# Attention's first microseconds: clears written as 32-bit pairs, centroids scaled by ScalarE, and a new set of ranks for the planner

## The chip, the core and the metric

The kernel runs on one core of a Trainium2 chip. A core has five engines that run side by side, each with its own queue, which it works off in order: TensorE (PE in the profile; its weight loads are shown apart as PEld), VectorE (DVE), ScalarE (ACT), GpSimd (POOL) and SyncE (SP), which here issues the DMAs. The engines work on a memory called SBUF; TensorE writes its results to a second one, PSUM, from which VectorE and ScalarE copy them. The metric is the time of one execution on the device, in microseconds.

## What is computed

A clustered attention with 4 batches, 8 heads, 768 positions and 64 features, followed by a mixture of 8 experts on its output, with gates made doubly stochastic in eight rounds.

```python
q_assign = argmax(q_n @ c_n, -1)      # nearest of 16 centroids, per head
k_assign = argmax(k_n @ c_n, -1)
mask = q_assign[:, :, :, None] == k_assign[:, :, None, :]
scores = where(mask, scale * q @ k.T, -1e9)
attn = exp(scores - max(scores)); attn /= sum(attn) + 1e-9
x = (attn @ v)                        # 3072 x 512
P = exp(x @ w_gate - max)             # eight rounds of row and column normalising
out = sum over e of P[:, e] * (relu(x @ w1[e]) @ w2[e])
```

## The kernel before

Attention comes first and lasts until about 486 us; the experts fill the rest with a fixed, hand-written order on TensorE that the change does not touch.

Attention goes by pairs of heads, 16 in all. Per pair: q and k are loaded (`load_pair`), transposed by TensorE and copied out of PSUM (`split_part`, L630 and L638), the sum of magnitudes gives a scale (`scale_pair`, L654 on ScalarE or L656 on VectorE, then small VectorE steps L659 to L665), and each is split into a high and a low 16-bit half (`split_pair`, L679 or L681, and L683). `assign_pair` multiplies q and k with the scaled centroids (L702) and turns the nearest cluster into 16 extra rows of the operands qX and kX, so that two positions of different clusters get a large negative score. Small DMAs (`place_pair`) put the halves in place. Per head, `max_chunk` forms scores in nine chunks of 512 columns and VectorE takes the maxima (L849, L853), `max_rows` makes rows of them, and `exp_chunk` forms the scores again with the maxima subtracted (L945, L946), ScalarE exponentiates (L952) and GpSimd adds up (L970). `values` multiplies with v (L1004), `norm` divides.

The upper 64 partitions of qX and kX, into which those extra rows go, must be filled before: with zero for q, with -32768 for k. There are 16 such buffers of 64 x 768 16-bit numbers. `clear` writes one on GpSimd (L421), or `clear_rest` does it on ScalarE (L461); `blank` zeroes seven other tiles (L448 on GpSimd, L450 on ScalarE). The same process loads ScalarE's table for the exponential by a dummy activation (L465) after the first four clears. Before the planner starts, the centroids are loaded, their norm is taken (L354 to L362, with a square root on ScalarE, L359 and L360), and VectorE scales them into both halves of `cs` (L365), which TensorE transposes (L373) and VectorE copies to `cm` (L377). Casts of the identity matrix for later transpositions are L205 and L207.

The order of attention's work is made when the program is built. A `Planner` holds, for each engine, the time at which it is free, and processes (Python generators) that ask for an engine and a duration, or for one of several (engine, duration, reluctance). At each step it looks for the step with the smallest start plus reluctance; among the steps of that engine that could start within the engine's PATIENCE of it, the one with the smallest key goes first. Keys come from `urgency`: nine per head, plus the stage's number in KEYS. The order that comes out is fixed on each engine; the true times are the chip's.

```python
start = max(w.time + self.latency(w.engine, on), self.free.get(on, 0.0))
...
steps.append((start, start + (o[2] if len(o) == 3 else 0.0), w.key, i, w, o, on))
...
first = min(steps, key=lambda x: x[1:4])
```

Of the kernel before, what the change touches and what calls it, by code (L numbers as in the profile page):

```python
# [8 lines left out]
F32 = mybir.dt.float32  # L9
# [4 lines left out]
AF = mybir.ActivationFunctionType  # L14
ALU = mybir.AluOpType
# [4 lines left out]
SHIFT = 2.0**15  # L20
# [40 lines left out]
class Planner:  # L61
# [3 lines left out]

    LATENCY = 0.2
    SHARING = ("POOL", "DVE+")
    PATIENCE = {'PE': 0.0, 'ACT': 0.0, 'POOL': 0.26, 'SP': 0.0, 'DVE': 0.0}

    def __init__(self, tc):  # L70
        self.tc = tc
# [58 lines left out]
    def run(self):  # L130
        while True:
# [16 lines left out]
            engine = first[6]  # L148
            last = first[1] + self.PATIENCE.get(engine, 0.0)
            start, _, _, _, w, cost, _ = min((x for x in steps if x[6] == engine and x[1] <= last), key=lambda x: (x[2], x[1], x[3]))  # L150
# [14 lines left out]
def attn_moe_kernel(  # L165
# [11 lines left out]
    nc = tc.nc  # L177
    B, H, S, D = q.shape
# [29 lines left out]
    ones = const.tile([P, P], F32, name="ones")  # L208
# [20 lines left out]
    PE, ACT, DVE, POOL, SP, DVE2 = "PE", "ACT", "DVE", "POOL", "SP", "DVE+"  # L229
# [104 lines left out]
    with ExitStack() as actx:  # L334
# [16 lines left out]
        cn = nat.tile([P, D], F32, name="cn", bufs=1)  # L351
# [3 lines left out]
        cnorm = sm.tile([P, 1], F32, name="cnorm", bufs=1)  # L355
        nc.vector.tensor_reduce(out=cnorm, in_=csq, axis=AX, op=ALU.add)
        root = sm.tile([P, 1], F32, name="root", bufs=1)
        begun = sm.tile([P, 1], F32, name="begun", bufs=1)
# [3 lines left out]
        nc.vector.reciprocal(cnorm, cnorm)  # L362
        cs = nat.tile([P, 2, D], F32, name="cs", bufs=1)
        for x in range(2):
            nc.vector.tensor_scalar(out=cs[:, x, :], in0=cn, scalar1=cnorm, scalar2=None, op0=ALU.mult)  # L365
        cm = const.tile([P, NP, 2, C], F32, name="cm")
        nc.vector.memset(cm.rearrange("p a x c -> p (a x c)"), 0.0)

# [47 lines left out]
        for nm, i in last:  # L416
            t = (pers if (nm, i) in kept else brief).tile([P, 2, S], F16, name=f"{nm[0]}{i}")
            for j in range(2):
                bufs[nm[j]].append(t[:, j, :])
        def clear(nm, t):  # L420
            nc.gpsimd.memset(t[64:128, :], -SHIFT if nm[0] == "k" else 0.0)  # L421


        def buffers(p):
# [17 lines left out]
        def blank(*ts):  # L442
            for t in ts:
                t = t if len(t.shape) == 2 else t.rearrange("p a b -> p (a b)")
                n = t.shape[1]
                e = yield (ACT, 0.08 + n * 0.00083), (POOL, 0.1 + n * 0.00083, RELUCT[10])
                if e == POOL:
# [2 lines left out]
                    nc.scalar.activation(t, ones[:, 0:1].broadcast_to([P, n]), AF.Copy, scale=0.0)  # L450

        def clear_rest():
            yield 6.0
            for i in range(NB):
                for nm, ts in bufs.items():
                    if "X" in nm and i < len(ts):
                        e = yield (ACT, 0.72), (POOL, 0.73, RELUCT[10])
                        if e == POOL:
                            clear(nm, ts[i])
                        else:  # L460
                            nc.scalar.activation(ts[i][64:128, :], ones[64:128, 0:1].broadcast_to([64, S]), AF.Copy, scale=-SHIFT if nm[0] == "k" else 0.0)  # L461
                ev["clear", i].set(plan)
                if i == 0:
                    yield ACT, 1.5
                    nc.scalar.activation(begun, begun, AF.Exp, scale=0.0)  # L465
                if i == 1:
                    yield from blank(nhs[0], ves[0], nhs[1])
                    ev["clear", "first"].set(plan)
            yield from blank(nhs[2], ves[1], *rrs, spread.rearrange("p t x d -> p (t x d)"))
            ev["clear", "rest"].set(plan)  # L470
            yield DVE2, 0.3
            three12 = sm.tile([3 * R, R], F32, name="three12", bufs=1)
            nc.vector.tensor_tensor(out=three12, in0=ident[0 : 3 * R, 0:R], in1=ident[0 : 3 * R, R : 2 * R], op=ALU.add)
            nc.vector.tensor_tensor(out=three12, in0=three12, in1=ident[0 : 3 * R, 2 * R : 3 * R], op=ALU.add)
            yield ACT, 0.75
            nc.scalar.copy(
                spread[0 : 3 * R], three12.rearrange("r (x i) -> r i x", x=2).unsqueeze(3).broadcast_to([3 * R, NT, 2, D])
            )
            ev["spread"].set(plan)
# [3 lines left out]
        xq_from, xs_from = ({n: next(free) for n in ns} for ns in (XQ, XS))  # L483
        NCH = len(CHUNKS)
        plan = Planner(tc)
        plan.free.update({PE: 5.0, ACT: 4.0, DVE: 6.3, POOL: 3.0, SP: 1.0})

        KEYS = dict(load=-99.6, scale=-39.4, hilo=-210.9, split0=-186.4, split1=-28.7, split2=-30.4, assign=-39.2, place=-336.7, chain=-64.9, ones=-461.5, max=-25.1, rows=-30.6, exp=0, values=64.8, out=6.0, batch=29.5, group=76.9, vsum=-28.1, group0=-123.5, inputs=-41.6, first=1000)
        NL = 32
        GATES = [0, 0, 1, 0]  # L490
        COSTS = [0.66, 0.46, 0.432, 0.214, 0.42]
        RELUCT = [4.75, -0.72, 2.33, 16.21, 0.34, 0.01, 0.02, 5.4, -0.46, 3.06, 0.07]

        FIRST = ("load", "split0", "split1", "split2", "scale", "hilo", "assign", "place", "chain", "ones", "max", "rows")

        def urgency(stage, n, c=0):
            return n * NCH + c + KEYS[stage] - (KEYS["first"] if n == 0 and stage in FIRST else 0)

# [954 lines left out]
    sink, making, scanning, inputs = gates(), iter(()), iter(()), iter(())  # L1453
# [3 lines left out]
    with ExitStack() as ax:  # L1457
# [124 lines left out]
        for t in range(NI):  # L1582
            e, f2 = divmod(t, NP2)
# [11 lines left out]
            if t == 8:  # L1595
                inputs = next_x(1, True)
# [263 lines left out]
    inputs = iter(())  # L1860
    for n in range(NS + 1):
        one = layer1b(n) if n < NS else iter(())
        two = layer2b(n - 1) if n else iter(())
        if n < NS:
            b, e = slots[n]
            if e == 1 and b + 1 < B:
                inputs = next_x(b + 1)
# [37 lines left out]
```

## Time and profile before

| | us |
|---|---|
| median of 3 runs | 2281.86 (2281.69 to 2282.4) |
| the profiled execution | 2279.16 |
| its span, first to last instruction | 2277.1 |
| TensorE busy in the span | 2236.1 |
| VectorE, ScalarE, GpSimd busy | 1649.1, 1143.1, 1118.1 |

A line of the profile names the line of the kernel, the engine, the operation, and what it writes and reads. A wait is put down to the event that came last. The chain of waits follows the work that ended last back in time, from each instruction to the one that released it.

### The profile page before, as it was taken

The page shows a single profiled execution, that of the slowest core. Times are in us where ns is not written, and L with a number is a line of the kernel's source. Part 1 is how long each engine was busy: PE and PEld are TensorE (multiplying, and loading weights), DVE is VectorE, ACT ScalarE, POOL GpSimd, SP SyncE. Part 2 cuts the span into 40 slices and gives each one's busy share as a digit, 9 for nine tenths or more (in the row PEclk, how much of TensorE's full clock was granted, in tenths as well). Part 3 has the DMA queues.
Part 4 walks back from the last instruction along what each step waited for, and adds up shares of the span by engine and source line. Part 5 has one row for each costly group of instructions (what it writes and reads, how often), then busy time and mean ns, then how long its engine had stood idle before and what let it go on. Part 6 is the DMA issues. An engine that isn't in the chain of part 4 may idle for free.

```text
span 2277.1 us, 39662 instructions
## 1 busy us (share of the span) xinstructions
PE 2236.1 (98%) x15491; PEld 1458.8 (64%) x15491; DVE 1649.1 (72%) x2777; ACT 1143.1 (50%) x2107; POOL 1118.1 (49%) x997
## 2 busy tenths in 40 slices
PE   6999999999999999999999999999999999999999
PEld 3455554445555555567777777777777777777777
DVE  7988878567666766588788877776676666666667
ACT  7777786555666665354444443333433333333333
POOL 3676787854555655276666653233332332322223
PEclk7999999999999999999999999999999999999999
DMA  5345453365555543586766765544444554434433
GB/s 128 88 101 159 103 142 98 124 218 198 186 168 190 190 139 111 203 300 210 223 218 218 239 219 169 176 144 132 151 156 141 182 170 139 131 130 132 138 130 102
DMA packets 226860, 369.78 MB, mean 162 GB/s; under 512 B 73800, under 2 KB 163824, under 8 KB 226160
## 3 DMA queue, kind: packets, MB, share of 16 engines
q1 hardware_dynamic: 226240, 365.67, 50.3%
q8 instruction: 121, 1.98, 0.4%
q10 hardware_dynamic: 432, 1.57, 0.2%
q14 instruction: 67, 0.55, 0.1%
HBM read 272.22 MB, written 80.62 MB: 155 GB/s over the span
## 4 chain that ended last, share of the span: by engine, by line
PE 91%; DVE 6%; ACT 2%; issue 1%; DMA 1%; SPq 0%; DVEq 0%; ACTq 0%
PE h_ps L1387 38%; PE pb L1805 12%; PE pa L1805 8%; PE pc L1805 8%; PE av_ps L1004 4%; PE o_ps L1547 4%; PE o_ps L1549 4%; PE o_ps L1548 4%; PE exp_ps L945 2%; PE max_ps L849 2%; PE exp_ps L946 2%; DVE mrt L853 2%; PE misc_ps L1045 1%; PE misc_ps L630 1%; ACT pe L952 0%
## 5 line engine op out<-in xcount | busy, mean ns | idle before, releaser
L1387 PEld LDWEIGHTS <-wa 128*128 128x128 f16 x5376 | 525.6, 98 | 302.8 <-issue 5.3
L1805 PEld LDWEIGHTS <-ho 128*128 128x128 f16 x5940 | 580.8, 98 | 137.2 <-DVE ho L1700 1.1
L1387 PE MATMUL h_ps<-xsT,wa 128*128 128x384 f16 x3072 | 581.6, 326 | 1.2 <-DVE xsT L324 0.6
L1387 PE MATMUL h_ps<-xsB,wa 128*128 128x384 f16 x2304 | 436.9, 326 | 1.4 <-DVE B L1401 0.6
L1681 POOL TENSOR_TENSOR B<-B,B 128x768 f32<-128x768 f32 x96 | 197.9, 2064 | 468.2 <-DVE ho L1700 426.6
L1700 DVE TENSOR_TENSOR ho<-B,ho 128x768 f16<-128x768 f32 x283 | 348.1, 1230 | 1.6 <-ACT ho L1696 1.6
L1851 ACT ACTIVATE B<-B 128x384 f32<-128x384 f32 x288 | 149.7, 520 | 371.3 <-DVE B L1401 370.0
L1805 PE MATMUL pb<-w2o,ho 128*128 128x256 f16 x2532 | 322.2, 273 | 0.0
L1401 DVE SCALAR_TENSOR_TENSOR u<-h_ps,m 128x384 f32<-128x384 f32 x256 | 141.7, 553 | 243.5 <-PE h_ps L1387 240.7
L1696 ACT CAST ho<-B 128x768 f16<-128x768 f32 x283 | 226.8, 824 | 14.1 <-POOL B L1681 13.4
L970 POOL TENSOR_TENSOR psum<-psum,pe 128x512 f32<-128x512 f32 x160 | 208.1, 1317 | 43.6 <-ACT pe L952 40.3
L853 DVE TENSOR_REDUCE mrt<-max_ps 128x1 f32<-128x512 f32 (+1 forms) x288 | 188.8, 683 | 41.0 <-PE max_ps L849 39.7
L1805 PE MATMUL pc<-w2o,ho 128*128 128x256 f16 x1692 | 215.7, 273 | 0.3
L1805 PE MATMUL pa<-w2o,ho 128*128 128x256 f16 x1692 | 215.1, 273 | 0.0
L1681 POOL TENSOR_TENSOR B<-B,T 128x768 f32<-128x768 f32 x48 | 95.6, 1991 | 206.0 <-DVE ho L1700 206.0
L952 ACT ACTIVATE pe<-exp_ps 128x512 f32<-128x512 f32 x288 | 164.8, 597 | 56.9 <-PE exp_ps L946 51.2
L1411 ACT ACTIVATE m<-h_ps 128x384 f32<-128x384 f32 x128 | 62.6, 489 | 191.6 <-PE h_ps L1387 190.8
L1849 ACT ACTIVATE B<-h_ps 128x384 f32<-128x384 f32 x96 | 47.1, 490 | 211.4 <-PE h_ps L1387 211.4
L1549 PE MATMUL o_ps<-wb,hl 128*128 128x512 f16 x384 | 145.5, 379 | 0.0
L1548 PE MATMUL o_ps<-wb,hh 128*128 128x512 f16 x384 | 145.5, 379 | 0.0
L1547 PE MATMUL o_ps<-wb,hh 128*128 128x512 f16 x384 | 145.5, 379 | 0.0
L1610 ACT ACTIVATE hh<-c 128x384 f16<-128x384 f32 x128 | 66.9, 523 | 143.2 <-DVE c L1401 142.0
(281 smaller groups left out, 3280.8 us busy)
## 6 DMA issues: line engine op xcount, KB each, us to landing
wa<-w1d SPq DMA_DIRECT2D x98, 896.0 KB
w2o<-w2d SPq DMA_DIRECT2D x168, 512.0 KB
raw<-in_moe_w SPq DMA_DIRECT2D x60, 512.0 KB
w1d<-wa SPq DMA_DIRECT2D x30, 896.0 KB
r<-in_moe_w SPq DMA_DIRECT2D x32, 512.0 KB
w2d<-w2s SPq DMA_DIRECT2D x32, 512.0 KB
w2d<-wb SPq DMA_DIRECT2D x96, 128.0 KB
scan<-in_moe_w SPq DMA_DIRECT2D x32, 256.0 KB
```

The costliest lines, as they stand in the source:

```text
L853: nc.vector.tensor_reduce(out=t["mr"][:, i0 : i0 + ni, ni - 1], in_=ps.rearrange("p (x c) -> p x c", x=ni), axis=AX, op=ALU.max)
L952: nc.scalar.activation(pe, ps.rearrange("p (x c) -> p x c", x=ni), AF.Exp, scale=SCALE)
L970: (nc.gpsimd if e == POOL else nc.vector).tensor_tensor(out=st[:, o : o + N0], in0=old[o], in1=part, op=ALU.add)
L1387: nc.tensor.matmul(ps[:, 0:HB], wa[:, w_, a, c, :], x[:, x_, c, :], start=(first and s_ == 0), stop=(s_ == len(steps) - 1), skip_group_che ...
L1547: nc.tensor.matmul(po[i], hh[:, t, ti], wbh[:, t], start=(first and t == 0), stop=False)
L1548: nc.tensor.matmul(po[i], hh[:, t, ti], wbl[:, t], start=False, stop=False)
L1549: nc.tensor.matmul(po[i], hl[:, t, ti], wbh[:, t], start=False, stop=(last and t == 1))
L1681: nc.gpsimd.tensor_tensor(out=t, in0=d[a], in1=d[c], op=ALU.subtract)
L1696: nc.scalar.copy(t[:, 0], blocks[n, g][o])
L1700: nc.vector.tensor_tensor(out=t[:, 1], in0=blocks[n, g][o], in1=t[:, 0], op=ALU.subtract)
L1805: nc.tensor.matmul(ps[q], h[:, h_, f, q * P : (q + 1) * P], w[:, 2 * g + f, w_], start=(first and g == 0 and s_ == 0 and q % 2 == 0), stop ...
L1851: rests.append(lambda: nc.scalar.activation(c, c, AF.Relu))
```

## The change

- The clears of qX and kX write 384 32-bit numbers where they wrote 768 16-bit ones. Their value for k is the 32-bit number whose two halves are both -32768.
- The two scalings of the centroids move from VectorE to ScalarE, and the dummy activation that loads the exponential's table moves from `clear_rest` to a place right behind them.
- `clear_rest` no longer begins with a delay of 6.0 in the plan's time, and the durations that it asks for are shorter.
- The planner is given other times at which ScalarE, VectorE and GpSimd are first free, another PATIENCE, other KEYS and other reluctances. RELUCT[10] is that of GpSimd for the clears and blanks, [2] that of VectorE for the sums of L970, [4] and [5] those of ScalarE and VectorE for the high halves, [6] that of VectorE for the magnitudes, [7] that of VectorE for the copies out of PSUM, [8] and [9] those of VectorE and GpSimd for the sums of v.

```diff
-    PATIENCE = {'PE': 0.0, 'ACT': 0.0, 'POOL': 0.26, 'SP': 0.0, 'DVE': 0.0}
+    PATIENCE = {'PE': 0.01, 'ACT': 0.16, 'POOL': 0.28, 'SP': 0.0, 'DVE': 0.15}
...
         for x in range(2):
-            nc.vector.tensor_scalar(out=cs[:, x, :], in0=cn, scalar1=cnorm, scalar2=None, op0=ALU.mult)
+            nc.scalar.activation(cs[:, x, :], cn, AF.Copy, scale=cnorm)
+        nc.scalar.activation(begun, cs[:, 1, 0:1], AF.Exp, scale=0.0)
...
+        PAIR = -(2.0**113) * (1 + 0xF800 / 2.0**23)
+        assert SHIFT == 2.0**15
+
         def clear(nm, t):
-            nc.gpsimd.memset(t[64:128, :], -SHIFT if nm[0] == "k" else 0.0)
+            nc.gpsimd.memset(t[64:128, :].bitcast(F32), PAIR if nm[0] == "k" else 0.0)
...
         def clear_rest():
-            yield 6.0
             for i in range(NB):
                 for nm, ts in bufs.items():
                     if "X" in nm and i < len(ts):
-                        e = yield (ACT, 0.72), (POOL, 0.73, RELUCT[10])
+                        e = yield (ACT, 0.42), (POOL, 0.38, RELUCT[10])
                         if e == POOL:
                             clear(nm, ts[i])
                         else:
-                            nc.scalar.activation(ts[i][64:128, :], ones[64:128, 0:1].broadcast_to([64, S]), AF.Copy, scale=-SHIFT if nm[0] == "k" else 0.0)
+                            nc.scalar.activation(
+                                ts[i][64:128, :].bitcast(F32), ones[64:128, 0:1].broadcast_to([64, S // 2]), AF.Copy, scale=PAIR if nm[0] == "k" else 0.0
+                            )
                 ev["clear", i].set(plan)
-                if i == 0:
-                    yield ACT, 1.5
-                    nc.scalar.activation(begun, begun, AF.Exp, scale=0.0)
...
-        plan.free.update({PE: 5.0, ACT: 4.0, DVE: 6.3, POOL: 3.0, SP: 1.0})
+        plan.free.update({PE: 5.0, ACT: 6.2, DVE: 6.2, POOL: 2.7, SP: 1.0})
 
-        KEYS = dict(load=-99.6, scale=-39.4, hilo=-210.9, split0=-186.4, split1=-28.7, split2=-30.4, assign=-39.2, place=-336.7, chain=-64.9, ones=-461.5, max=-25.1, rows=-30.6, exp=0, values=64.8, out=6.0, batch=29.5, group=76.9, vsum=-28.1, group0=-123.5, inputs=-41.6, first=1000)
+        KEYS = dict(load=324.0, scale=-43.9, hilo=-165.9, split0=-88.0, split1=-58.3, split2=-42.9, assign=-26.7, place=-255.2, chain=-60.4, ones=-533.3, max=-24.1, rows=-117.3, exp=0, values=56.1, out=18.8, batch=-218.8, group=210.8, vsum=-143.1, group0=-194.2, inputs=-302.1, first=1000)
...
-        RELUCT = [4.75, -0.72, 2.33, 16.21, 0.34, 0.01, 0.02, 5.4, -0.46, 3.06, 0.07]
+        RELUCT = [32.96, -4.19, 3.07, -0.21, 0.33, 3.81, 1.36, 0.59, 0.16, 5.81, -8.55]
```

## Rows read from the trace of the kernel before

**Rows 1.** The page's first part: busy time, share, instructions of TensorE.

```profile
PE 2236.1 (98%) x15491; PEld 1458.8 (64%) x15491; DVE 1649.1 (72%) x2777; ACT 1143.1 (50%) x2107; POOL 1118.1 (49%) x997
```

**Rows 2.** Busy time by stretch; the stretch and its length come first.

```profile
core 0: us, PE busy (x) PEld busy (x) DVE busy (x) ACT busy (x) POOL busy (x), PEclk, DMA share, GB/s
...
8.00:40.50 32.50, 20.09 (x80) 9.13 (x79) 26.84 (x60) 23.82 (x41) 0.91 (x4) 0.64 0.44 100
40.50:60.00 19.50, 18.40 (x115) 9.99 (x114) 13.30 (x25) 17.13 (x34) 14.16 (x15) 0.98 0.65 145
60.00:160.00 100.00, 94.79 (x625) 49.66 (x625) 87.74 (x171) 74.37 (x175) 70.11 (x85) 1.00 0.39 93
160.00:200.00 40.00, 39.10 (x254) 20.76 (x253) 39.06 (x76) 30.44 (x72) 30.89 (x38) 1.00 0.63 166
200.00:486.00 286.00, 278.00 (x1833) 138.02 (x1832) 210.57 (x403) 199.78 (x477) 216.77 (x261) 1.00 0.42 117
```

**Rows 3.** The timeline from 0 to 14: start, duration, engine, line.

```profile
2.24 1.57 ACT L461 ACTIVATE qX<-ones 64x768 f16<-64x768 f32 x2
...
2.67 4.13 POOL L421 MEMSET qX<- 64x768 f16 x6
...
3.84 0.20 ACT L360 ACTIVATE root<-cnorm 128x1 f32<-128x1 f32 x1
...
4.46 2.42 DVE L365 TENSOR_SCALAR cs<-cn,cnorm 128x64 f32<-128x64 f32 x2
...
4.79 2.16 DVE L205 CAST ident_h<-ident 128x128 f16<-128x128 f32 x1
...
6.85 0.77 POOL L448 MEMSET nht<- 128x768 f32 x1
...
7.27 1.06 PE L630 MATMUL misc_ps<-ident,qn 128*128 128x128 f32 x4
...
8.08 0.44 DVE L377 COPY cm<-misc_ps 64x64 f32<-64x64 f32 x2
...
9.13 1.49 PE L630 MATMUL misc_ps<-ident,kn 128*128 128x128 f32 x6
```

**Rows 4.** The chain of waits up to 41: shares by line, then pieces.

```profile
by line: ACT qX L461 14.0%; DVE mrt L853 8.7%; DVE cs L365 5.9%; PE max_ps L849 4.8%; PE misc_ps L630 4.7%; ACT qn L638 4.7%; DVE qH L683 4.5%; ACT nht L450 3.6%; ACT L359 3.1%; ACT L465 3.1%; DVE qX L758 2.7%; PE misc_ps L702 2.7%; issue 2
...
10.23 1.28 ACT L465
...
11.52 0.20 ACT begun L465
...
12.87 0.59 ACT kn L638
...
13.51 1.09 PE misc_ps L702 x6
...
16.27 0.74 ACT nht L450
...
40.48 0.43 PE exp_ps L945
```

**Rows 5.** Line 638: duration in ns (least, median, most), first and last start.

```profile
L638 ACT COPY qn<-misc_ps x32: 344/489/606, 8.4 to 337.7; 128x512 f32<-128x512 f32 x16, 128x256 f32<-128x256 f32 x16
...
L638 ACTq EVENT_SEMAPHORE  x17: 17/17/17, 5.2 to 319.0; - x17
```

**Rows 6.** Instructions by line up to 486: busy us, mean ns, idle before.

```profile
L853 DVE TENSOR_REDUCE mrt<-max_ps 128x1 f32<-128x512 f32 (+1 forms) x288 | 188.8, 683 | 41.0 <-PE max_ps L849 39.7
...
L656 DVE TENSOR_REDUCE am<-qn 128x1 f32<-128x768 f32 x7 | 6.6, 946 | 4.8 <-ACT qn L638 4.8
...
L1131 DVE COPY gt<-misc_ps 96x256 f32<-96x256 f32 x3 | 1.3, 421 | 3.1 <-PE misc_ps L1125 3.1
...
L421 POOL MEMSET qX<- 64x768 f16 x6 | 4.1, 731 | 0.1
```

**Rows 7.** Who waited for whom on TensorE, 40 to 486: us, times, longest.

```profile
PE max_ps L849 <- DVE mrt L853: 5.0, 11, 1.4
```

## The prediction

> **What bounds the kernel now.** I read the page's first part first [rows 1]: TensorE is busy for 2236.1 of 2277.1 us. The table of stretches says where most of the other 41 us lie [rows 2]: from 8 to 40.5 it is busy 20.09 of 32.5 us, and before 8 there is hardly a matmul in the timeline [rows 3]; from 40.5 to 486, where attention ends, it is busy 430.3 of 445.5. Everything later is a fixed order on a full TensorE, and the diff leaves it alone. So the change is worth what it moves the point at which TensorE fills up, the first exponential chunk, at 40.48 in the chain of waits [rows 4], plus or minus what the new ranks do to the 15.2 us still idle between there and 486.
>
> Then the timeline of the start [rows 3] and the chain up to 41 us [rows 4]. ScalarE is the engine to watch: of those 41 us the chain passes 14.0% through its clears L461 (5.7 us), 3.1% through the exponential's table L465 (1.3 us, and 0.20 for the activation behind it), 3.31 us through six pieces of its blanks L450 (the first stands in the rows), and 5.9% through VectorE's scaling of the centroids L365 (2.4 us). That is 12.9 us of work on which no result of this stretch depends directly, or that is long only because it stands blocked. GpSimd, meanwhile, is busy for 0.91 of 32.5 us between 8 and 40.5 [rows 2]. VectorE is the next in line: 26.84 of the same 32.5 us, so 5.7 us idle.
>
> **The change, part by part.**
>
> Centroids. The reader sees two delays in [rows 3]: the root L360 stands behind two clears on ScalarE (2.24 to 3.84), and then both L365 need 2.42 us, since they start at 4.46 inside GpSimd's row of clears and end at 6.88, just after the row's end at 6.80. Afterwards ScalarE has no clears to do: root right after the sum of squares (about 3.0), two small VectorE steps (0.4 in all, from 4.04 to 4.46 before), two ScalarE copies of 128x64, each between the 0.20 of the 128x1 root and the 0.59 of a copy of 512 columns; I take 0.25, near the former, whose size is nearer. The scaled centroids are there at about 4.1 in place of 6.88. TensorE's queue begins with their transposition, and q's transpositions stand behind it (7.27); q has landed at 5.2, when the first of ScalarE's waits for a load is over [rows 5]. So q starts 2.0 us earlier, bounded by its landing, and 0.7 of the 2.8 us are lost to that.
>
> Table. L465 (1.28 + 0.20) leaves the chain at 10.23 and goes behind the copies, 4.1 to 5.6. It is hidden there by q's landing and its four transpositions, which end at about 6.3; without that cover it would cost 1.5. In this trace the next activation starts 0.01 us after the load [rows 4]. The Trainium skill (ScalarE: Activation LUTs, What ACT_TABLE_LOAD costs) gives 1283 ns for the load, with which the trace agrees, and another 1380 ns of drain, which it does not show; with that the first copy of q would be some 0.7 us late and the sum 5.8 in place of 6.5.
>
> Clears and blanks. In the planner's choice an engine's start counts plus its reluctance; at -8.55 GpSimd is preferred for all of them, because the process that issues them is one behind the other and never finds ScalarE 8.55 us ahead. So ScalarE loses 10 clears and 7 blanks. GpSimd's cost goes by elements, not bytes: 768 columns took 0.73 us as 16 bits [rows 6] and 0.77 as 32 bits [rows 3], so 384 pairs cost about 0.38. Sixteen are 6.1 us; three blanks of 768 columns and smaller ones of some 1.0 us in all are 3.3. GpSimd is busy from 2.67 to about 12.1 and has nothing else to do until the first rows' end.
>
> What that row of writes does to VectorE is this change's danger. The cast L205, queued at 4.79, ended at 6.95 [rows 3]. The six clears of 0.73 [rows 6] took 4.13 together, so each starts before the one before has ended, and nothing of VectorE's gets in between; the blank L448, of another shape, starts at 6.85, after a short pause, and the three waiting VectorE instructions passed there. Afterwards this pause comes after eight short clears, at 2.67 + 8 x 0.38 = 5.7. The casts (a second one follows) pass there, the small ones behind them take 0.4, and VectorE copies the transposed centroids at about 6.2 in place of 8.08. The Trainium skill (SBUF — State Buffer, Who interferes with whom) says that the one that starts first holds the shared ports for its whole instruction and the other blocks fully. By that sentence alone a cast would slip in after one clear, at about 4; this trace shows that it waits for three of them. Copies at 4.6 in place of 6.2 would help little, as k is not there yet: some 0.3 us, and the sum would be 6.8.
>
> The sum. *Up to the raw q and k*: on the chain between 8.37 and 15.7 stand two clears and the table, 0.84 + 0.84 + 1.48 = 3.2 us [rows 4]. With the 2.0 before them that would be 5.2. But k has to land: its time is not shown, it lies between 5.2, since it is issued behind q, and 9.1, when TensorE used it [rows 3]; I take 7, the middle. Then k's transpositions, copies and the rest end at about 10 in place of 13.46: 3.5 us. *From there to 40.5*: what is left of the 12.9 on the chain are clears and blanks of 5.8 us. What is late next is VectorE: it has 5.7 us idle in the whole stretch. Some of it belongs to the wait for q and k that is already counted, and some stays, since the first head's maxima go to and fro between VectorE and a TensorE that is partly at 1.2 GHz (0.64 of 2.4 granted on the mean from 8 to 40.5, 0.98 after [rows 2]). I take 3.0, about half. Together 6.5: the first exponential at about 34.
>
> Bounds: below, VectorE idles as much as before and only starts 1.9 us earlier; above, all 12.9 less 0.5 for the copies, if the second pair's VectorE work (some 5 us done before 40.5) is left for later. TensorE's clock came up where it got dense; it should do so that much earlier, which is in the sum.
>
> Ranks and patience from 40.5 to 486. They touch all of attention, and no row of before prices an order. The idle TensorE time there is 15.2 us; a better order gains no more, a worse one may lose as much. The reluctances shift work: copies out of PSUM, all on ScalarE now (32 of q [rows 5], and as many of k), become cheap for VectorE (5.4 to 0.59), sums of magnitudes (7 of q's 16 on VectorE [rows 6]) and the high halves become dear there. These roughly balance, so I take 0 and carry 4 either way into the range. Loads fall far back (-99.6 to 324) on SP's queue, behind the placing DMAs; they run pairs ahead, so nothing waits for a few us.
>
> The profiled execution took 2279.16 us (span 2277.1), 2.7 under the median of 2281.86. 2279.16 - 6.5 = 2272.7; against the median, 2275.4.
>
> **Rivals.**
> *The lock.* GpSimd's row has no pause that VectorE can use until 12.1; casts, centroid copies and all behind them start at 12.2. For it: the cast of before ended only with the row. Against it: the pause at 6.80. The assignment, which ended at 14.6 before [rows 4], waits for the centroids until 12.8, and with its 8 matmuls ends hardly sooner; nothing is left of the 3.5, and the lighter ScalarE still gives some 2: 2280, no change.
> *VectorE becomes the bound*, the one that ends slower. It has 87.7 of 100 and 39.06 of 40 us from 60 to 200 [rows 2]. A copy of 512 columns lies between the 0.42 of a 256-column one and the 0.68 of a 512-column reduction [rows 6]; both sizes for both inputs are about 2 us a pair, and a pair's copies come every 21 us (8.4 to 337.7 for 16 pairs [rows 5]). If most copies go to VectorE with little taken off it, two pairs' 4 us fill its 5.7 idle ones before 40.5, so the start gains nothing, and 13 us in 60 to 200 meet 13.2 idle ones. From there on every maximum makes TensorE wait: about 6 us, 2288. Against it: the magnitudes and high halves that leave.
> *Given back.* The start gains 6.5, and the new order leaves TensorE waiting that much more up to 486: most likely where it waits now, for the maxima (5.0 us [rows 7]), 2281, no change. For it: the ranks change everywhere; against: TensorE is 97% busy there under either.
>
> **How the numbers follow.** Forecast 0.60, lock 0.13, VectorE bound 0.13, given back 0.14. What a measurement of this kernel can tell from no change is about 0.2%, 4.6 us. The forecast's own range is 2270 to 2279; nine tenths of it gain over 4.6. The range for all is 2268 (12.4 and a little of the order) to 2283, which leaves out the VectorE case and the tail of the forecast. Faster 0.55, within 0.2% 0.31 (the rest of the forecast, the lock, most of what is given back), slower 0.14.
>
> **What would show it.** No clear or blank on ScalarE, 16 clears of about 0.38 us on GpSimd; scaled centroids at about 4, table load before 6; q's transpositions at 5.3; centroid copies at about 6 (12 is the lock); the first exponential at 33 to 36; TensorE's busy time from there to attention's end as before, with 15 us idle. If VectorE is over 95% busy from 60 to 200, or copies sit on it in numbers, it is the second rival; an early first exponential with an unmoved end of attention is the third.

## The result, and the profile of the changed kernel

The changed kernel takes 2293.93 us (median; 2291.11 to 2297.4) where the kernel before, timed beside it, takes 2282.4 (2281.69 to 2284.11). The ratio is 1.0051, 95% interval 1.0036 to 1.0066: slower by half a per cent, where I had forecast 2275.4 and a gain. The profiled execution took 2297.4 us (span 2295.6), the longest of its kernel, and that of before 2279.16, a short one. So the two traces lie 18 us apart and the medians 11.5; what follows explains the 18, and about a third of it is the two executions.

The page's first part shows the same instructions on TensorE as [rows 1] and 12.0 us more of its time.

```profile
PE 2248.1 (98%) x15491; PEld 1462.2 (64%) x15491; DVE 1656.1 (72%) x2777; ACT 1141.4 (50%) x2106; POOL 1116.9 (49%) x1009
```

The beginning came as forecast. The timeline of the changed kernel (start, duration, engine, line) answers [rows 3]:

```profile
2.66 2.93 POOL L425 MEMSET qX<- 64x384 f32 x8
...
3.50 2.18 DVE L205 CAST ident_h<-ident 128x128 f16<-128x128 f32 x1
3.62 0.59 ACT L365 ACTIVATE cs<-cn,cnorm 128x64 f32<-128x64 f32 x2 [0.42 <-DVE cnorm L362]
...
4.22 1.28 ACT L366 ACT_TABLE_LOAD   x1
...
5.53 1.11 PE L632 MATMUL misc_ps<-ident,qn 128*128 128x128 f32 x4 [0.74 <-DMA qn<-in_q]
5.65 0.77 POOL L452 MEMSET nht<- 128x768 f32 x1
...
6.16 0.44 DVE L378 COPY cm<-misc_ps 64x64 f32<-64x64 f32 x2
```

ScalarE has no clear left, eight clears take GpSimd 2.93 us, the centroids are scaled at 3.62 to 4.21, the table's load ends at 5.50 and q's transpositions start at 5.53, VectorE's casts end in GpSimd's pause at 5.68, and the centroid copies stand at 6.16 (8.08 before). The first exponential's matmul, by the instructions that write its tile (count, least, median and longest ns, first and last start), first in the changed kernel, then in the kernel before:

```profile
L947 PE MATMUL exp_ps<-qH x192: 269/376/634, 33.4 to 483.8; 128*128 128x512 f16 x96, 128*128 128x256 f16 x96
```

```profile
L945 PE MATMUL exp_ps<-qH x192: 269/330/634, 40.3 to 470.9; 128*128 128x512 f16 x96, 128*128 128x256 f16 x96
```

33.4 us in place of 40.3: 6.9 us sooner. The same query for the first product of expert 0's second layer, in the same order:

```profile
L1549 PE MATMUL o_ps<-wb,hh x384: 376/379/379, 512.8 to 972.8; 128*128 128x512 f16 x192
```

```profile
L1547 PE MATMUL o_ps<-wb,hh x384: 376/379/379, 494.3 to 954.4; 128*128 128x512 f16 x192
```

512.8 in place of 494.3, so 18.5 us later. From there to the end both kernels need the same: 2295.6 - 512.8 = 1782.8 and 2277.1 - 494.3 = 1782.8. The whole difference, and 6.9 us more, arises between the first exponential and this product. By stretches (the stretch, its length, busy time of each engine, granted clock) the changed kernel answers [rows 2] so:

```profile
8.00:40.50 32.50, 23.04 (x94) 10.24 (x93) 26.30 (x56) 16.66 (x31) 6.15 (x18) 0.72 0.50 108
...
60.00:160.00 100.00, 90.06 (x567) 47.38 (x565) 88.34 (x175) 69.25 (x155) 60.69 (x82) 0.97 0.44 99
160.00:200.00 40.00, 39.32 (x262) 19.73 (x262) 32.00 (x62) 33.24 (x82) 29.64 (x36) 1.00 0.39 99
200.00:486.00 286.00, 277.98 (x1799) 137.73 (x1799) 214.23 (x399) 197.84 (x475) 214.45 (x256) 0.99 0.43 119
486.00:510.00 24.00, 17.21 (x106) 8.40 (x102) 16.38 (x26) 10.76 (x20) 3.50 (x4) 0.86 0.66 218
```

and the kernel before has in the last of these

```profile
486.00:510.00 24.00, 23.50 (x136) 12.72 (x134) 20.73 (x51) 11.62 (x20) 7.46 (x8) 1.00 1.03 355
```

From 8 to 40.5 TensorE does 3 us more, from 60 to 160 it is idle for 9.9 us where 5.2 were, and from 486 to 510 for 6.8 where 0.5 was. VectorE is no busier than before (88.34 of 100, then 32.00 of 40 where it had 39.06).

Idle time is only part of it. The granted clock, 1.00 after 41.3 us in the profiled execution of before, falls to 1.2 GHz four more times here:

```profile
0.00:512.80 512.80, 471.12 (x2954) 236.11 (x2955) 398.05 (x767) 350.19 (x806) 337.39 (x431) 0.96 0.45 119
18.60:25.50 6.90, 4.97 (x23) 2.12 (x24) 6.06 (x13) 2.11 (x4) 0.00 (x0) 0.51 0.45 105
28.90:42.50 13.60, 10.96 (x40) 5.45 (x40) 10.82 (x24) 7.45 (x12) 3.52 (x6) 0.50 0.40 78
83.50:90.30 6.80, 4.70 (x17) 2.32 (x18) 6.35 (x12) 2.35 (x4) 0.72 (x1) 0.50 0.25 59
223.40:226.80 3.40, 3.40 (x10) 0.98 (x10) 1.54 (x3) 2.17 (x4) 0.00 (x0) 0.50 0.26 63
305.30:308.80 3.50, 3.50 (x11) 1.03 (x12) 3.15 (x11) 2.96 (x7) 3.42 (x7) 0.51 0.24 39
493.10:499.90 6.80, 5.76 (x35) 2.69 (x35) 4.78 (x7) 3.43 (x6) 0.40 (x1) 0.50 0.55 169
```

```profile
0.00:494.30 494.30, 459.15 (x2953) 232.74 (x2954) 389.36 (x767) 352.27 (x807) 339.79 (x419) 0.98 0.46 120
14.00:17.40 3.40, 3.36 (x15) 1.86 (x9) 2.25 (x10) 2.62 (x7) 0.00 (x0) 0.50 0.00 0
20.80:41.30 20.50, 12.52 (x47) 4.78 (x47) 17.70 (x38) 13.21 (x24) 0.91 (x4) 0.50 0.45 102
```

Up to that first product TensorE was idle for 512.80 - 471.12 = 41.7 us, before for 494.30 - 459.15 = 35.2: 6.5 more, although the beginning is shorter. At 1.2 GHz it worked for 33.3 us (the sum of the six short stretches) where it had 15.9: 17.4 more, half of which, 8.7, is what the lower clock adds to these instructions. 6.5 + 8.7 is 15.2 of the 18.5 us; the other 3.3 lie in longer matmuls that these rows don't split further. The 8.7 belong to this pair of executions, whose mean granted clocks are 0.991 and 0.995. The median executions are closer: 0.993 for the changed kernel, and 0.993 to 0.995 for the kernel before as it ran beside the experiments. A thousandth of 2280 us is 2.3, so of the 11.5 us between the medians the clock adds at most some 5 (an estimate). Ahead of each of the four later falls stands a stretch in which TensorE was idle: it was busy for 1.45 of the 3.5 us before 83.5, for 6.76 of the 8.4 before 223.4, for 3.67 of the 5.3 before 305.3 and for 4.68 of the 7.1 before 493.1. The first and the last of these:

```profile
80.00:83.50 3.50, 1.45 (x11) 0.59 (x8) 3.26 (x13) 2.32 (x6) 0.46 (x3) 1.00 0.37 88
```

```profile
486.00:493.10 7.10, 4.68 (x33) 2.14 (x29) 2.27 (x5) 3.02 (x7) 3.10 (x4) 1.00 0.31 93
```

What TensorE waited for from 60 to 100 us (us in total, times, longest):

```profile
PE max_ps L851 <- DVE mrt L855: 2.9, 8, 1.1
PE misc_ps L778 <- DVE om L771: 2.6, 1, 2.6
PE misc_ps L1085 <- ACT rr L1078: 1.3, 1, 1.3
```

```profile
PE max_ps L849 <- DVE mrt L853: 1.3, 3, 0.9
PE misc_ps L1045 <- DVE ms L588: 0.9, 1, 0.9
```

TensorE waits for the maxima (mrt), for the next pair's mask (om) and for a normalisation (rr); its queue is a fixed order, so nothing passes ahead of the instruction that waits. It is not that an engine has more to do there: from 60 to 100 us VectorE is busy for 36.98 us (37.81 before) and ScalarE for 24.10 (30.26). Nearly the same instructions stand in another sequence. That the sequence is the cause, these rows only suggest.

### The profile page after: what moved, and what is told of

Read it like the earlier page. It is cut to its first block, busy times and chain, and to the rows that moved or that the text cites. A ratio compares the mean times of both kernels' runs of the same rounds, so it can differ in the third digit from the quotient of the medians.

```text
span 2295.6 us, 39687 instructions
## 1 busy us (share of the span) xinstructions
PE 2248.1 (98%) x15491; PEld 1462.2 (64%) x15491; DVE 1656.1 (72%) x2777; ACT 1141.4 (50%) x2106; POOL 1116.9 (49%) x1009
## 4 chain that ended last, share of the span: by engine, by line
PE 90%; DVE 4%; ACT 1%; issue 1%; DMA 1%; POOL 0%; DVEq 0%; ACTq 0%
PE h_ps L1389 37%; PE pb L1807 12%; PE pa L1807 8%; PE pc L1807 8%; PE av_ps L1006 5%; PE o_ps L1551 4%; PE o_ps L1549 4%; PE o_ps L1550 4%; PE exp_ps L947 2%; PE max_ps L851 2%; PE exp_ps L948 2%; DVE mrt L855 1%; PE misc_ps L1047 1%; DMA scan<-in_moe_w 0%; DVE ho L1702 0%
## 5 line engine op out<-in xcount | busy, mean ns | idle before, releaser
L1698 ACT CAST ho<-B 128x768 f16<-128x768 f32 x283 | 226.9, 824 | 14.1 <-POOL B L1683 13.5
L1006 PE MATMUL av_ps<-pe,vn 128*64 128x512 f32 (+1 forms) x768 | 138.5, 502 | 0.7 <-ACT pe L954 0.7
```

Of the source, the lines that this page charges most:

```text
L1006: nc.tensor.matmul(av[o, a:z], vn[:, i, :], heads[t]["pe", c][:, i - i0], start=(i == 0), stop=False, skip_group_check=True)
L1698: nc.scalar.copy(t[:, 0], blocks[n, g][o])
```

## Experiments

The question is whether the 18 us belong to the new steps of the beginning, to the new order, or to the way the two meet. The first two kernels take the change apart crosswise: in each the plan is one kernel's, with all its durations, ranks and patience, and the instructions are the other's. Times are medians, ratios are to the kernel before on the same chip; the last two columns are starts in the profiled execution. That is one execution, up to some us off its median (of e1 1.8 above it, of the kernel before 3.2 below), so small differences in these columns are not differences of the medians.

| kernel | us | ratio (95%) | first exponential | first second-layer product |
|---|---|---|---|---|
| before | 2282.4 | 1 | 40.3 | 494.3 |
| changed | 2293.93 | 1.0051 (1.0036 to 1.0066) | 33.4 | 512.8 |
| e1 new steps, old order | 2278.74 | 0.9985 (0.9976 to 0.9994) | 36.8 | 496.5 |
| e2 old steps, new order | 2296.33 | 1.0063 (1.0049 to 1.0077) | 35.7 | 511.2 |
| e3 early weights sooner | 2295.62 | 1.0062 (1.0049 to 1.0076) | 34.2 | 513.0 |
| e4 new beginning, old ranks | 2305.03 | 1.0099 (1.0085 to 1.0113) | 37.4 | 519.9 |
| e5 ranks sought | 2277.28 | 0.9974 (0.9963 to 0.9984) | 36.2 | 493.2 |
| e6 one rank by one | 2302.59 | 1.0082 (1.0066 to 1.0097) | 40.7 | 517.3 |
| e7 scaling undone | 2279.24 | 0.9984 (0.9975 to 0.9993) | 36.6 | 492.6 |
| e8 table only, old order | 2281.96 | 0.9993 (0.9984 to 1.0002) | 38.6 | 497.4 |
| e9 clears only, old order | 2278.83 | 0.9985 (0.9976 to 0.9994) | 36.7 | 494.6 |
| e10 ranks sought, second set | 2280.01 | 0.9989 (0.9980 to 0.9998) | 35.1 | 494.5 |
| e11 ranks sought, third set | 2276.01 | 0.9969 (0.9959 to 0.9979) | 34.7 | 489.4 |

### The new steps in the old order

To the kernel before:

```diff
-            nc.vector.tensor_scalar(out=cs[:, x, :], in0=cn, scalar1=cnorm, scalar2=None, op0=ALU.mult)
+            nc.scalar.activation(cs[:, x, :], cn, AF.Copy, scale=cnorm)
+        nc.scalar.activation(begun, cs[:, 1, 0:1], AF.Exp, scale=0.0)
...
-            nc.gpsimd.memset(t[64:128, :], -SHIFT if nm[0] == "k" else 0.0)
+            nc.gpsimd.memset(t[64:128, :].bitcast(F32), PAIR if nm[0] == "k" else 0.0)
...
-                    nc.scalar.activation(begun, begun, AF.Exp, scale=0.0)
```

and ScalarE's clears by pairs in the same way; the plan's `yield`s and numbers stay.

> The new beginning's instructions (clears by 32-bit pairs on whichever engine took them, centroids scaled on ScalarE, the exponential's table loaded right behind, its later load gone) in the kernel before's plan: ranks, patience and the plan's durations are the old ones, so every planned step stands in its old place. Theory R (the new order of attention is what costs; the new steps by themselves pay): first exponential between 34 and 38 us instead of 40.28, the stretches 60 to 160 and 480 to 510 dense as before, time 2282.4 - 4 = 2278, between 2275 and 2280. Rival S (an earlier beginning is given back in the attention, whatever the order, because a later wait takes it): first exponential as early, time 2281 to 2284. Rival T (the new steps themselves do harm): over 2285.

Measured: 2278.74 us, a gain of 3.9 with an interval of 1.4 to 5.5 us. Theory R's time holds, and T falls: the steps do no harm. S, 2281 to 2284, is touched by the edge of the interval alone. From 60 us on TensorE is as dense as before:

```profile
60.00:100.00 40.00, 36.73 (x244) 19.65 (x242) 36.01 (x75) 30.74 (x72) 24.72 (x32) 1.00 0.33 76
...
480.00:510.00 30.00, 27.58 (x157) 13.78 (x155) 24.63 (x53) 13.48 (x25) 8.42 (x9) 0.89 0.87 299
```

In the kernel before these are 36.98 and 27.16. The one difference is the clock, 0.89 in the last stretch. This profiled execution took 2280.52 us at a mean clock of 0.992, and the shortest of the same kernel 2277.18 at 0.995: with one and the same order the clock falls more in one execution than in another.

### The old steps in the new order

To the changed kernel, the same edits backwards, with the exponential's first activation behind the first clears.

> The mirror of it: the changed kernel's plan (new ranks, patience and durations, so its order) with the old instructions in it: clears of 16-bit values, the two centroid scalings on VectorE, the exponential's table loaded after the first clears. Theory R: the whole loss stays and what the new steps gave (some 4 to 7 us) goes, so 2298 to 2301. Rival T (the new steps do the harm): back to 2281 to 2285. Rival S: the late beginning costs nothing, 2292 to 2295.

Measured: 2296.33 us. Rival T is out again: the loss stays when the steps go. It is 2.4 us above the changed kernel, short of the 4 to 7 that theory R wanted and above the 2292 to 2295 of rival S. One thing in it is not as before: the table load, which has no place of its own in the new plan, went ahead of the root, so that ScalarE loads two tables more (at 2.23 the exponential's, at 3.74 the root's again, and once more at the first exponential). In the stretch that is worst in the changed kernel it is the changed kernel's double, 31.22 against 31.21 us. First this kernel, then the changed one:

```profile
60.00:100.00 40.00, 31.22 (x187) 15.85 (x183) 37.00 (x78) 24.04 (x53) 12.70 (x23) 0.91 0.49 110
```

```profile
60.00:100.00 40.00, 31.21 (x184) 15.64 (x184) 36.98 (x79) 24.10 (x53) 12.76 (x23) 0.91 0.49 109
```

So the new order with new steps is slower than the old order with new steps by 15.2 us, and with old steps by 13.7 (2296.33 - 2282.63); the steps are worth 2.4 to 3.9 in either. The order is the cause. And it also makes much of the beginning: its first exponential comes at 35.7 even with the slow steps.

### Is it the change to the experts?

Much of the 18 us appears after 486 us, where the splits of the experts' first inputs wait for expert 0's weights. In the changed kernel:

```diff
-        plan.spawn(early_weights(), urgency("values", nheads - 12))
+        plan.spawn(early_weights(), urgency("values", nheads - 20))
```

> The changed kernel with one number changed: expert 0's early weights are spawned with the rank of values for head nheads-20 instead of nheads-12. The order up to about 340 us is the changed kernel's. Theory R1 (some 13 of the lost us are lost at the change from attention to the experts, 480 to 510 us, because the early weights end at 490 us and the experts' first inputs are split only behind them): the splits of the experts' inputs begin 10 to 30 us sooner, the clock does not fall at 493, time 2281 to 2286. Rival R2 (the attention's last heads themselves are late, and the experts' start waits for them whatever the weights do): within 2 us of the changed kernel, 2291 to 2296.

Measured: 2295.62 us; R1 falls. The weights did come sooner, and with them the first product of the experts, at 466.0 in place of 492.4:

```profile
L1389 PE MATMUL h_ps<-xsB,wa x2304: 323/327/337, 466.0 to 2262.4; 128*128 128x384 f16 x192
```

The clock did not fall at 493. But the work that went forward pushed the attention back (its last exponential starts on ScalarE at 492.8 in place of 484.7). TensorE now waited 4.8 us in one piece for an earlier pair's normalisation, from 435.2 to 440.0, and there the clock fell:

```profile
439.90:446.70 6.80, 6.55 (x25) 3.50 (x26) 2.49 (x5) 4.75 (x11) 4.93 (x4) 0.50 0.12 40
```

```profile
PE misc_ps L1085 <- ACT rr L1078: 5.5, 3, 4.8
```

The first second-layer product stands at 513.0, 0.2 us from where it was. The place where the loss shows was not its cause. Rival R2 had the time right; that it was the attention's last heads that set it is what these rows suggest, and it was not tried by itself.

### The old ranks for the new beginning

If the new ranks are bad numbers, the old ones should be better. The changed kernel with the old KEYS, PATIENCE (but TensorE's 0.01) and RELUCT (but the clears').

> The changed kernel with the old ranks, reluctances (all but the clears') and patience (all but TensorE's 0.01): the plan is made anew for the new beginning with the old numbers. Theory R in its simple form (the old ranks are good ones, the new ones bad): 2274 to 2279. Rival U (ranks are good only for the beginning they were chosen for; a plan made anew from an earlier beginning is another order, and most orders are worse than the kernel before's): slower than the kernel before, 2288 to 2305, with new idle stretches of TensorE in other places.

Measured: 2305.03 us, the slowest of all. The simple form of R falls, and U holds, at the upper end of its range. The idle time sits where neither kernel had it: from 100 to 160 TensorE is busy for 49.44 us (57.80 before, 58.85 in the changed kernel):

```profile
100.00:160.00 60.00, 49.44 (x297) 25.51 (x296) 50.38 (x101) 37.56 (x90) 30.02 (x44) 0.91 0.32 73
```

So the new ranks are not worse than the old ones: for this beginning they are 11 us better. The old ranks were good with the old beginning only.

### One rank by one

The kernel before, with nothing of the change but this:

```diff
-        KEYS = dict(load=-99.6, ..., max=-25.1, rows=-30.6, ...)
+        KEYS = dict(load=-99.6, ..., max=-24.1, rows=-30.6, ...)
```

> The kernel before with one number changed by one: the rank of the max stage -24.1 (the changed kernel's value) instead of -25.1, a twelfth of one head's rank. Beginning and instructions are untouched. Theory U (the order is a knife's edge: small changes of rank give other orders and most are worse): 2292 to 2306, first exponential unchanged at 40.3, new idle stretches of TensorE from 100 us on with falls of the clock. Rival R' (ranks act smoothly, a shift by one is worth about nothing, and the changed kernel's loss comes of its large shifts, load by 423, batch by 248, inputs by 260): 2281 to 2284.

Measured: 2302.59 us, 1.0082. R' falls. The beginning is the same (first exponential 40.7 against 40.3), up to 100 us TensorE is as busy as before (52.24 against 51.54 of 55), and then it falls behind (in the last stretch the kernel before is busy for 31.39 us). The first fence is this kernel, the second the kernel before, the third what TensorE of this kernel waited for from 100 to 200:

```profile
100.00:200.00 100.00, 93.03 (x589) 46.71 (x591) 84.22 (x154) 70.45 (x165) 68.69 (x82) 0.97 0.47 120
...
480.00:515.00 35.00, 28.44 (x166) 12.46 (x163) 16.25 (x23) 14.23 (x30) 18.88 (x15) 0.90 0.26 88
```

```profile
100.00:200.00 100.00, 96.91 (x635) 50.44 (x635) 88.99 (x167) 74.55 (x174) 76.39 (x91) 1.00 0.48 122
```

```profile
PE max_ps L849 <- DVE mrt L853: 2.7, 6, 0.9
PE exp_ps L945 <- ACT pe L952: 2.2, 3, 1.0
```

The waits are small ones spread over maxima and exponentials, with the loads of a later pair behind them (1.4 us), and the clock falls in both stretches (0.97 and 0.90), as in the changed kernel. A shift by 1 is one chunk, a ninth of a head (288 chunks in 32 heads; the expectation's twelfth is a slip). In one of some twenty ranks it costs more than the whole change.

### The scaling undone, the plan made anew

In the changed kernel the scaling goes back to VectorE and the table behind the first clears, with its step in the plan:

```diff
-            nc.scalar.activation(cs[:, x, :], cn, AF.Copy, scale=cnorm)
-        nc.scalar.activation(begun, cs[:, 1, 0:1], AF.Exp, scale=0.0)
+            nc.vector.tensor_scalar(out=cs[:, x, :], in0=cn, scalar1=cnorm, scalar2=None, op0=ALU.mult)
...
+                if i == 0:
+                    yield ACT, 1.5
+                    nc.scalar.activation(begun, begun, AF.Exp, scale=0.0)
```

> The changed kernel with the new ranks, clears by pairs, but the centroids scaled on VectorE again and the table loaded after the first clears, as before, with its step in the plan. The first exponential comes later, at 38 to 41 us. If the beginning sets the time (the theory of my prediction): slower than the changed kernel by 3 to 5, 2297 to 2299. Theory U (another step in the beginning gives another order, and its quality outweighs the beginning): time set by idle TensorE after 45 us, and this order packs closer: 2280 to 2288 in spite of the later first exponential.

Measured: 2279.24 us, 14.7 less than the changed kernel and 0.8 below theory U's range. The first exponential came at 36.6, sooner than I expected but 3.2 later than in the changed kernel, and the end 14.7 sooner. With the new ranks, one 1.5 us step put back in the plan gives an order in which TensorE is as busy after 45 us as in the kernel before (454.18 of 470 us). First this kernel (its shortest execution), then the changed one (its longest), then the kernel before:

```profile
45.00:515.00 470.00, 454.75 (x2954) 231.10 (x2952) 371.67 (x723) 339.47 (x782) 345.57 (x409) 1.00 0.48 134
```

```profile
45.00:515.00 470.00, 443.43 (x2841) 222.38 (x2840) 366.74 (x689) 326.99 (x761) 321.35 (x386) 0.98 0.45 120
```

```profile
45.00:515.00 470.00, 454.18 (x2964) 231.57 (x2963) 372.65 (x725) 331.84 (x772) 341.56 (x407) 1.00 0.48 133
```

### What the steps are worth

Two kernels split e1: only the scaling and the table, and only the clears, each in the old order.

> The kernel before with its order and its 16-bit clears, and only the centroids scaled on ScalarE and the exponential's table loaded right behind. It splits the gain of e1 (3.9 us). If the table and the scaling are worth most, as my prediction had it (3.5 us, the copies of the raw q and k no longer behind the late table and the two scalings): 2278.5 to 2280.5. If the clears are worth most: 2281 to 2283.

> The kernel before with its order, its centroid scalings and its late table, and only the clears by 32-bit pairs. With e1 at -3.9 us and e8 at -1.4: if the two parts add, 2280 to 2281.5 (-2.5). If the clears do nothing without the earlier table (a queue in ScalarE hides them), 2282.5 to 2284. If they are worth all of e1 by themselves, 2278 to 2280.

Measured: 2281.96 (0.9993, not to be told from no change) and 2278.83 (0.9985). The clears alone give all of e1; the scaling and the table add nothing to them that these runs can tell. The timeline shows why they don't add at the first copy of q. First the clears alone, then the table alone:

```profile
2.67 2.21 POOL L424 MEMSET qX<- 64x384 f32 x6
...
6.66 0.59 ACT L643 COPY qn<-misc_ps 128x512 f32<-128x512 f32 x1 [3.25 <-PE misc_ps L635]
```

```profile
4.44 0.59 ACT L365 ACTIVATE cs<-cn,cnorm 128x64 f32<-128x64 f32 x2 [0.42 <-DVE cnorm L362]
...
6.71 0.59 ACT L638 COPY qn<-misc_ps 128x512 f32<-128x512 f32 x1 [0.16 <-PE misc_ps L630]
```

Either brings the first copy of q from 8.37 to 6.7, and both together (6.73 in e1) bring no more: q's transpositions now start when q has landed, at 5.50, 5.55 and 5.58. Both undo the same delay: VectorE's scaling of the centroids stood blocked until GpSimd's row of clears ended. With short clears the row ends at 4.88 in place of 6.80; on ScalarE the scaling does not stand in it at all.

At the copies of k the two do add: the last one ends at 13.5 us before, at 11.2 in either kernel and at 9.7 in e1. But the first exponential keeps nothing of it (36.7 in e9, 36.8 in e1). The chain of waits up to 41 us shows another wait ahead of it. In the kernel before, the chain went through ScalarE [rows 4]; in all three it starts with the load of v, which lands at 10.4 in e9, 10.7 in e8 and 10.0 in e1. VectorE then sums over v for 2.9 us, and its fixed order has the scale of q and k behind that. The lines are of e9 and of e8:

```profile
2.85 7.50 DMA vn<-in_v
```

```profile
2.87 7.82 DMA vn<-in_v
```

What e9 has and e8 has not are ScalarE's shorter clears, 0.52 us in place of 0.84 each. That they make the 1.9 us between the two first exponentials is not shown.

### Other orders for the new beginning

Three sets of ranks, reluctances and patience for the changed kernel's beginning, sought by the plan's own durations; e11's is a neighbour of e5's. Of e11:

```diff
-        KEYS = dict(load=324.0, hilo=-165.9, assign=-26.7, rows=-117.3, values=56.1, inputs=-302.1, ...)
+        KEYS = dict(load=306.6, hilo=-120.6, assign=-44.7, rows=-284.3, values=38.0, inputs=62.3, ...)
```

> The changed kernel with ranks, reluctances and patience sought anew for its own beginning (most of them near the changed kernel's; rows, values, inputs, assign, hilo, place, chain and the reluctances for magnitudes and copies differ). Theory U (a set of ranks is good only as a whole and for one beginning; the new beginning pays as soon as an order is found that suits it): first exponential at 33 to 35 us, TensorE idle after 45 us no more than the 15 us of before, no fall of the clock after 45 us, time 2282.4 - 7 - 0 to 4, so 2270 to 2276. Rival S (the early beginning is given back in attention because a later resource binds): 2279 to 2284. Rival V (no order chosen by the kernel's own durations keeps its gain on the chip): 2285 to 2300.

> The changed kernel with another set of ranks sought for its beginning, from another path (scale 23 for -44, split0 -52, assign -58, values 45, vsum -58, inputs -170 and others). Theory U: a second order that suits the beginning also beats the kernel before, 2270 to 2279, with at most some 16 us of idle TensorE after 45 us. Rival V (e5 was a lucky one; orders chosen by the durations in the kernel scatter on the chip by as much as the rest): 2279 to 2300.

> A neighbour of e5's ranks (place, assign, values, vsum, inputs and three reluctances differ a little). Theory U: near e5, 2272 to 2280, if the order stays close to e5's; rival V: 2280 to 2300.

Measured: 2277.28, 2280.01 and 2276.01; all three are faster than the kernel before, e11 by 7.0 us (0.9969). Theory U's ranges held e11 alone; e5 missed by 1.3 us and e10 by 1.0, and e10's time is one that S and V allowed too. So V is not out: orders taken by the plan's own durations gain between 3 and 7 us. U also had no fall of the clock after 45 us in e5, and there was one (0.95 granted from 480 to 515). S falls in its general form, since one order keeps nearly the whole of the early beginning. In e11 the first exponential stands at 34.7 and TensorE is as dense afterwards as in the kernel before, 455.14 against 454.18 of the 470 us:

```profile
45.00:515.00 470.00, 455.14 (x2958) 231.55 (x2958) 371.81 (x728) 339.33 (x777) 345.82 (x411) 1.00 0.49 136
```

In the profiled executions e11 is 5.6 us ahead of the kernel before at the first exponential and still 4.9 at the first second-layer product; the medians differ by 7.0. In the two others the first exponentials came at 36.2 and 35.1.

## Why the prediction was wrong, step by step

**The beginning was right in its sum and wrong in its parts.** Forecast: the first exponential 6.5 us sooner, at about 34; measured 6.9 sooner, at 33.4. Landing, pause, casts, centroid copies and k (7.20, where I took 7) came within some tenths. But the last raw copy of k ends at 10.78 in place of 13.46, 2.7 us sooner where I had 3.5, and from there to the first exponential 4.2 were gained where I had 3.0. That the two errors cancel is luck. I bounded the first part by k's landing alone. In the changed kernel v lands at 10.2, VectorE sums over it first, and the scale of q and k starts at 12.99 in place of 14.46; I had no term for that. e1 and e2 show that the new instructions bring the first exponential 3.5 us forward in the old order and 2.3 in the new one. The rest of the 6.9 comes with the new plan, which also takes the clears and blanks off ScalarE.

**The step that failed is "Ranks and patience from 40.5 to 486", of which I said "so I take 0 and carry 4 either way into the range".** Two sentences above it I had the bound, 15.2 us of idle time that a worse order might lose once more, and then used a quarter of it, for no reason in a row. e2 against the kernel before (13.7), and the changed kernel against e1 (15.2), put the net price of the new order at 14 to 15 us. The same order brings the first exponential forward by 4.6 us (40.3 - 35.7) and 3.4 (36.8 - 33.4), so what it loses behind that, the term itself, is 18.3 to 18.6 us where I took 0 (times by the medians, starts by the profiled executions). I weighed the change of ranks by what each moves on its engine (copies to VectorE, loads far back), found that these balance, and took that for the price of an order. They did balance: only 10 of the raw copies went to VectorE, and it is hardly busier than before (1656.1 us in all, 1649.1 before). The price came from elsewhere. A list planner decides each step by what is free at that moment, so one other decision changes all later ones; e6 shows 19 us from a shift by 1, e7 15 us from a step of 1.5 us. No balance of engines sees that.

**I also let the order end at 486.** "Everything later is a fixed order on a full TensorE, and the diff leaves it alone" is right from the first second-layer product on (1782.8 us in both). Between 486 and there stand the experts' first inputs, whose splits and weights have ranks too; there TensorE lost 6.3 us of busy time in 24. e3 filled that place, and the time did not fall.

**The clock had a price that I gave only to the beginning.** I counted on the clock for the first 41 us. In the new order it fell again after four loose stretches, and in the profiled pair 8.7 of the 18.5 us are that (17.4 us of work at 1.2 GHz in these stretches); between the medians it is at most some 5. So an idle microsecond can cost more than one. The 15.2 us were no bound on what a worse order can lose: the term measured 18.3 to 18.6.

**Rivals.** The lock: out, the casts passed in the pause at 5.65 as forecast. VectorE as the bound: out by its own mark (88% and 80% busy from 60 to 200, where it said 95), although the maxima are once more what TensorE waits for most. Given back: its mechanism, TensorE waiting more in a new order, is the one that happened, and it was priced at the size of the gain, 6.5, with no reason that it should stop there. It had 0.14 and no tail on the slow side; the range's upper end, 2283, left out all of it. What I argued against it, "TensorE is 97% busy there under either", was what had to be shown.

## What to carry to other kernels

A list plan with tuned ranks belongs to the very durations that it was tuned on: when one step changes, keep the old order with the new instructions first (here a gain of 3.9 us), and treat new ranks as a second change that is not to be priced engine by engine. For a prediction, an order that no row prices carries at least the stretch's whole idle time on the losing side, since neighbours of a tuned order can be far worse (e4, e6) and the falling clock can add to a gap. Two delays that end at the same event are one term of the sum, and when both go, the next wait in line, here the landing of v, is the bound.

## What the runs showed of the hardware

**VectorE's casts end with GpSimd's whole row of clears**, however long it is: the row of eight 16-bit clears in e2 ends at 8.15 and the cast L205 at 8.30; six 16-bit ones end at 6.80 and the cast at 6.95 [rows 3]; eight short ones in the changed kernel at 5.59 and it at 5.68; six short ones in e1 at 4.88 and it at 4.96. The lines of e2:

```profile
2.66 5.49 POOL L421 MEMSET qX<- 64x768 f16 x8
...
5.99 2.31 DVE L205 CAST ident_h<-ident 128x128 f16<-128x128 f32 x1
```

The Trainium skill (SBUF — State Buffer, Who interferes with whom) has the one that starts first holding the shared ports for its whole instruction; here the cast waited for the whole row of one shape, in all four. That it is the ports which are held so long, no run here shows.

**GpSimd's clears go by elements**: 64x384 pairs took 2.93 / 8 = 0.37 us each and 768 16-bit values 5.49 / 8 = 0.69. This I had expected; that it alone makes the gain of the beginning in the old order (e9) I had not.

**The clock falls in one execution of an order and not in another.** e1 and the kernel before have one order; e1's profiled execution shows 1.2 GHz in part of 480 to 510 and that of before none. Nor does the mean clock of an execution settle its time: the kernel before took 2281.96 us at 0.999 and 2281.99 at 0.993, and the eleven executions of e10, at 0.991 to 0.998, all took 2278.9 to 2281.22. What makes the clock fall in one of them and not in another, these runs don't show.
